# A fused attention and two gated MLPs on one core: the first MLP's token chunks resized, its first chunk fed unnormalised

## The chip, the cores and the metric

The kernel runs on one core of one Trainium2 chip, as one launch. The metric is the device time in microseconds (us) of that core, the median over several executions. Lower is better. The engines are named as in the profile: PE (matrix multiply), PEld (its weight loads, a separate row), DVE (VectorE), ACT (ScalarE), POOL (GpSimd), SP (the queue that issues the DMAs).

## The reference

The input is attention with two kinds of masks, whose output goes through two gated MLPs:

```python
scores = scale * q @ k^T        # batch 4, heads 8, 576 positions, head size 64
# heads 0-3 see the last 32 positions; heads 4-7 every 4th of the last 128
attn_out = softmax(masked scores) @ v
x = attn_out as [2304 tokens, 512]
xn = x / sqrt(mean(x*x, axis=-1) + 1e-6) * rms_g
x  = (silu(xn @ w_gate) * (xn @ w_val)) @ w_out            # 512 -> 1536 -> 512
out = (sigmoid(x @ w_gate2) * (x @ w_val2)) @ w_out2
```

Inputs and outputs are float32; the MLP weights arrive as 64-bit words whose two halves are combined into a float32 on the chip.

## The kernel before

**Numbers.** Every float32 operand of an MLP product is split into a high part that the matrix engine holds exactly (float32r) and the rest. A product is then three matmuls with stationary operands hi, hi, lo (lines 1362 and 1442); each matmul loads its own 128x128 stationary operand.

**First MLP.** The 1536 hidden units are 12 blocks of 128. HOLDS = (6, 6): a first half (pass 0) runs all tokens through blocks 0 to 5, whose weights stay in SBUF, and a second half (pass 1) runs all tokens through blocks 6 to 11 and adds the partial sums. Each half walks over chunks of tokens, `SIZES` in pass 0 and `WIDE` in pass 1, both six chunks of 384. One step of `mlp_step` (one block, one chunk) is 12 matmuls for the gate into bank g, 12 for the value into bank v, an activation and a product on ACT and DVE, and a split into `h`; `y_group` adds 12 matmuls of the step before into four banks y0 to y3. So a chunk costs 6 x 36 = 216 matmuls of the chunk's width, and a half over six chunks 1296.

**Attention and norm.** Attention runs in 48 groups (batch, pair of heads, third of the sequence) that are spread over pass 0. `plan_attention` puts before each chunk the groups that its tokens need: all three groups of the two dilated pairs of every batch that the chunk touches, and the groups of the plain pairs that its tokens lie in. For the six chunks of 384 that is 10, 10, 4, 10, 10, 4 groups. Then `x_norm` squares, sums (line 1067), takes a reciprocal root (lines 1083 to 1108), turns it back by PE (line 1124), scales (line 1147) and splits the chunk (lines 582 to 589). `x_store` writes the split chunk to DRAM for pass 1, one DMA per plane of 128 features and per wide chunk that it overlaps.

**Loads.** q and k of the four pairs of batch 0 come token-major and are turned by PE (`first_qk`, line 796, 16 transposes of 72x72 for one pair, copied out on ACT or DVE). The pairs of the other batches come by `attn_load`: eight DMAs of 72 KB (line 902) and two transposes on DVE (line 916). With `by_pe` = n the first n of those pairs go by `first_qk` instead. MLP weights come through a ring of three buffers `wst` (lines 542, 546): ACT takes an absolute value (line 563), DVE combines the words in four instructions (lines 566, 569, 572, 575), and ACT, POOL or DVE split the result. A `wst` buffer is free when line 575 has read it.

**Second MLP.** It works by a seven-product block scheme on 288-column halves of each batch (lines 1670 and 1593), with sums on DVE, and is not touched.

**Order.** `Line.emit` is a list scheduler that runs when the program is built. It knows engine costs, buffer rings and due times and writes out a fixed order for each engine and for SP. All weights, due times and biases of it are in the dictionary `PARAMS`; `fill_from`, `fill_gap` and `fill_share` say when it puts matmuls on zeros in front of a matmul that it expects to wait.

**Switches that are off before.** With `raw0`, the first chunk isn't scaled by the norm. `plain_split` splits gain times x, and the norm's row is applied behind the products, in pass 0 and once more in pass 1 for the same tokens (a copy of the row is kept in DRAM):

```python
nc.vector.tensor_tensor(out=q.t[:, 0:raw], in0=row.t, in1=gb.t[:, 0:raw], op=ALU.mult)
if raw < T1:
    nc.vector.tensor_copy(out=q.t[:, raw:], in_=gb.t[:, raw:])
...
add("PL", pool(raw), lambda: nc.gpsimd.tensor_tensor(
    out=t.t[:, 0:raw], in0=t.t[:, 0:raw], in1=row.t, op=ALU.mult),
    reads=[("row", "rowm")[p]], writes=[key], tiles=[t, row], due=s + 3.7 * mul,
    other=("x0_lo", "DVE", dves(raw), ...))
```

Chunks of pass 1 that are wider than 384 take parts of their tiles from a second pool (`broad`); nothing else of the arithmetic changes with them.

Of the kernel before, what the change touches and what calls it, by code (L numbers as in the profile page):

```python
# [21 lines left out]


PARAMS = {
    "late": 0, "fill_share": -1.519, "fill_max": 6, "gather": 0.866, "w0_hi": 17.594,
    "w0_lo": 13.068, "h0_hi": 0.512, "h0_lo": -0.096, "x0_hi": 0.96, "x0_lo": 1.138, "ahead": 2,
    "todo0": 464.368, "todo1": 9.635, "todo2": 47.212, "todo3": 0.618, "xb_zero": -1.082,
    "stay": 0.104, "phase": 1.6, "fill_from": 7.028, "fill_gap": -3.039, "margin": 2139.515,
    "wait": 1.172, "w_sq": 3.146, "w_hi": 0.024, "w_lo": 0.907, "x_hi": 0.265, "x_lo": 0.0,
    "h_hi": 7.774, "h_lo": 0.002, "qk": 0.304, "norm": 0.51, "pts": 8.696, "o": 0.0, "snap": 6.738,  # L30
    "h_ahead": 8.667, "h2_ahead": 0.956, "evac": 7.026, "holds": (6, 6), "norm_act": 1.016,
    "slack": 0.0, "share_v": 0.6, "share_p": 0.33, "cold": 1.7, "low": 0, "high": 0.39,
    "recip": 0.3, "rel1": 106.122, "span1": -0.902, "rel2": 17.835, "span2": -0.521, "ys": 0.468,
    "ts": 0.415, "cross": 0.06, "same": 0.04, "dma_lat": 1.7, "dma_rate": 330000.0, "by_pe": 0,
# [3 lines left out]
    "ld_v": -61.445, "ld_c": -66.281, "ld_d": -14.37, "lead": 1.181, "xdue": 12.095,  # L38
    "wdue": -1.028, "wslope": 2.786, "wload": -341.212, "wload_step": 9.03, "warm_n": 36,
    "warm_t": 0.889, "warm_dt": 0.03, "warm_c": 19, "warm_m": 5, "warm_late": -3.526,  # L40
    "warm_due": 32.425, "mask_cost": 0.18, "exp_cost": 0.36, "s_cost": 0.546, "o_cost": 0.41,
    "t_cost": 0.265, "pt_lead": 8.027, "x_lead": 12.171, "wy_due": -0.031, "y_from": 7.985,
    "y_step": 1.502, "xb_due": 0.362, "y_last": 1.346, "xb_last": 6.045, "lo6": 114.359,
    "hi6": 18.752, "sizes": (384, 384, 384, 384, 384, 384), "wide": (384, 384, 384, 384, 384, 384),
    "rush": -0.629, "rush_to": 0.301, "raws": 1, "turns": 2, "raw0": 0,
}
STEP = 6.24

# [1905 lines left out]
```

## Time and profile before

| | us |
|---|---|
| median of 3 runs (1004.35 to 1007.39) | 1005.12 |
| the profiled execution | 1005.76 |
| its span, first to last instruction | 1004.0 |
| PE busy in the span | 974.6 |
| PEld / DVE / ACT / POOL busy | 946.2 / 732.4 / 478.3 / 405.8 |

A busy share is the share of time in which at least one instruction of the engine was in flight. For PE it hides two things: the pipe's latency behind a short burst, and the clock that was granted, which is either 1.2 or 2.4 GHz and is shown as a share of full speed. A stretch with PE busy at a granted clock of 0.80 has 40% of its time at the lower level.

### The profile page before, as it was taken

What the parts mean: (1) busy time and instruction counts of PE and PEld (TensorE: products, weight loads), DVE (VectorE), ACT (ScalarE), POOL (GpSimd) and SP (SyncE); (2) the same over time, 40 slices, a digit from 0 to 9 for tenths busy, and PEclk for the clock granted to TensorE, in tenths of its full rate; (3) what the DMA queues carried; (4) which work ended last, traced back from release to release, by engine and by line L of the source; (5) the groups of instructions that cost most, each with busy time, mean ns of one, the idle gap of its engine ahead of it and who ended that gap; (6) DMA issues with size and microseconds to landing.
All of it is one profiled execution on the core that took longest, in us unless ns stands there. A gap on an engine that the chain in (4) does not pass through costs nothing. (4 is left out here: it accounts for less than half of the span.)

```text
span 1004.0 us, 20084 instructions
## 1 busy us (share of the span) xinstructions
PE 974.6 (97%) x7096; PEld 946.2 (94%) x7096; DVE 732.4 (73%) x1712; ACT 478.3 (48%) x1305; POOL 405.8 (40%) x602
## 2 busy tenths in 40 slices
PE   7898899999999999999999999999999999999997
PEld 6678798998999999999999999999999999999996
DVE  6787897867886888744432569778977688788766
ACT  5976657646432443222221336546654455454432
POOL 5663874443433640010000457337753037661111
PEclk8789799999999999999999999999999999999999
DMA  8858698676779687974662455545276463547634
GB/s 205 191 148 179 134 288 222 155 214 183 236 232 311 228 278 240 331 252 176 234 220 88 136 162 190 210 183 173 69 259 212 156 225 124 189 151 236 161 79 93
DMA packets 213252, 194.53 MB, mean 194 GB/s; under 512 B 137312, under 2 KB 178848, under 8 KB 213152
## 3 DMA queue, kind: packets, MB, share of 16 engines
q1 hardware_dynamic: 213152, 193.25, 63.5%
q8 instruction: 56, 0.92, 0.4%
q14 instruction: 44, 0.36, 0.1%
HBM read 129.50 MB, written 63.70 MB: 192 GB/s over the span
## 5 line engine op out<-in xcount | busy, mean ns | idle before, releaser
L1442 PE MATMUL y<-h,wo 128*128 128x384 f32 x864 | 167.9, 340 | 0.5 <-DVE h L589 0.4
L1362 PE MATMUL g<-xo,w 128*128 128x384 f32 x864 | 165.7, 340 | 0.0
L1362 PE MATMUL v<-xo,w 128*128 128x384 f32 x864 | 162.9, 336 | 0.0
L1442 PEld LDWEIGHTS y<-h,wo 128*128 128x128 f32 x864 | 150.5, 189 | 2.5 <-DVE h L589 0.7
L1362 PEld LDWEIGHTS g<-xo,w 128*128 128x128 f32 x864 | 152.2, 191 | 0.3
L1362 PEld LDWEIGHTS v<-xo,w 128*128 128x128 f32 x864 | 150.2, 188 | 1.3
L582 ACT CAST h<-t 128x384 fp32r<-128x384 f32 (+1 forms) x139 | 65.7, 473 | 111.9 <-DVE t L1410 86.3
L586 POOL TENSOR_TENSOR h<-t,h 128x288 fp32r<-128x288 f32 (+1 forms) x45 | 42.0, 934 | 156.6 <-ACT h L582 151.2
L1410 DVE TENSOR_TENSOR t<-t,v 128x384 f32<-128x384 f32 x72 | 39.6, 550 | 64.0 <-PE v L1362 63.3
L1542 DVE SCALAR_TENSOR_TENSOR pt<-y,pt 128x288 f32<-128x288 f32 x133 | 60.0, 452 | 36.0 <-PE y L1593 33.3
L974 POOL TENSOR_SCALAR pr<-pr,rs 128x96 f32<-128x96 f32 x132 | 57.1, 446 | 56.3 <-DVE rs L969 44.0
L589 DVE TENSOR_TENSOR h<-t,h 128x384 fp32r<-128x384 f32 (+1 forms) x95 | 58.5, 616 | 24.9 <-ACT h L582 23.9
L1593 PE MATMUL y<-h,wo 128*128 128x288 f32 x399 | 72.7, 295 | 0.3 <-ACT h L582 0.2
L586 POOL TENSOR_TENSOR w<-wz,w 128x256 fp32r<-128x256 f32 x58 | 47.3, 830 | 48.5 <-ACT w L582 35.2
L563 ACT ACTIVATE wz<-wst 128x512 f32<-128x512 f32 x72 | 47.9, 669 | 35.1 <-DMA z<-wz 21.7
L1593 PEld LDWEIGHTS y<-h,wo 128*128 128x128 f32 x399 | 59.5, 188 | 0.8 <-ACT h L582 0.5
L586 POOL TENSOR_TENSOR w<-S,w 128x256 fp32r<-128x256 f32 x48 | 38.7, 820 | 52.2 <-DVE w L584 38.0
L572 DVE SCALAR_TENSOR_TENSOR wz<-wst,wz 128x512 int32<-128x512 int32 x72 | 55.8, 775 | 0.9
L961 ACT ACTIVATE pr<-pr,nmx 128x96 f32<-128x96 f32 x144 | 52.4, 366 | 8.0 <-DVE nmx L955 7.7
L575 DVE SCALAR_TENSOR_TENSOR wz<-wst,wz 128x512 int32<-128x512 int32 x72 | 53.2, 738 | 0.6
L1696 ACT ACTIVATE t<-t 128x288 f32<-128x288 f32 x72 | 31.9, 444 | 45.5 <-DVE t L1687 43.9
L586 POOL TENSOR_TENSOR x<-t,x 128x288 fp32r<-128x288 f32 x29 | 27.2, 942 | 64.3 <-ACT x L582 64.3
(231 smaller groups left out, 2112.8 us busy)
## 6 DMA issues: line engine op xcount, KB each, us to landing
z<-wz SPq DMA_DIRECT2D x54, 256.0 KB, 4.7
xo<-xs SPq DMA_DIRECT2D x23, 576.0 KB, 5.7
wst<-in_moe_w_gate_dram SPq DMA_DIRECT2D x24, 512.0 KB, 4.6
wst<-in_moe_w_val_dram SPq DMA_DIRECT2D x24, 512.0 KB, 5.4
wst<-in_moe_w_out_dram SPq DMA_DIRECT2D x24, 512.0 KB, 5.4
xs<-xs SPq DMA_DIRECT2D x21, 576.0 KB, 2.8
wst<-xs SPq DMA_DIRECT2D x18, 576.0 KB, 5.3
x<-xo SPq DMA_DIRECT2D x24, 384.0 KB, 3.2
```

The source lines that it names most:

```text
L563: add("ACT", act(CW), lambda: nc.scalar.activation(out=z.t.bitcast(F32), in_=top().bitcast(F32), func=ACTF.Abs), reads=[("wst", key)], wri ...
L572: add("DVE", Shared(0.595), lambda: nc.vector.scalar_tensor_tensor(out=z.t, in0=top(), scalar=-0x40000000, in1=z.t, op0=ALU.bitwise_and, o ...
L575: add("DVE", Shared(0.595), lambda: nc.vector.scalar_tensor_tensor(out=z.t, in0=low(), scalar=29, in1=z.t, op0=ALU.logical_shift_right, op ...
L582: add("ACT", act(n), lambda: nc.scalar.copy(out=hi(), in_=src()), reads=reads, writes=[key] + [order] * bool(order), tiles=tiles + [dst], ...
L586: add("PL", pool(n), lambda: nc.gpsimd.tensor_tensor(out=lo(), in0=src(), in1=hi().bitcast(F32), op=ALU.subtract), reads=reads, writes=[ke ...
L589: other=(kind + "_lo", "DVE", dves(n), lambda: nc.vector.tensor_tensor(out=lo(), in0=src(), in1=hi().bitcast(F32), op=ALU.subtract)))
L961: add("ACT", PARAMS["exp_cost"], lambda u=u: nc.scalar.activation(out=pr.t[:, u], in_=pr.t[:, u], func=ACTF.Exp, bias=nmx.t[:, u:u + 1], s ...
L974: add("PL", Shared(0.305), lambda u=u: nc.gpsimd.tensor_scalar(out=pr.t[:, u], in0=pr.t[:, u], scalar1=rs.t[:, u:u + 1], scalar2=1.0, op0= ...
L1362: nc.tensor.matmul(out=bank.t, lhsT=w[:, l, cols], rhs=x, start=kk == order[0] and n == 0, stop=kk == order[-1] and n == 2)
L1442: nc.tensor.matmul(out=yb.t, lhsT=w.t[:, l, s], rhs=hs[r].t if broad(p, c) else hs[r].t[:, r], start=n == 0 and j == 0, stop=n == HOLDS[p] ...
L1542: add("DVE", dve(T), lambda: nc.vector.scalar_tensor_tensor(out=t.t[:, e, h], in0=bank.t, scalar=0.5, in1=t.t[:, e, h], op0=ALU.mult, op1= ...
L1593: nc.tensor.matmul(out=bank.t, lhsT=w.t[:, u, a, n], rhs=hs[u].t[:, d], start=first and u == 0 and m == 0, stop=u == NF // 2 - 1 and m == ...
```

## The change

Only `PARAMS` changes. The sizes and switches among it:

- pass 0 in seven chunks, 384, 192, 384, 384, 384, 384, 192, so that the second ends with batch 0 (token 576); the groups before the chunks become 10, 2, 10, 10, 4, 10, 2;
- pass 1 in five chunks, four of 512 and one of 256;
- `raw0` on; `by_pe` = 2, so that the two dilated pairs of batch 1 are turned by PE;
- the scheduler's weights and due times are other ones throughout, those for zero matmuls among them.

```diff
--- before.py
+++ after.py
-    "late": 0, "fill_share": -1.519, "fill_max": 6, "gather": 0.866, "w0_hi": 17.594,
+    "late": 0, "fill_share": -0.39, "fill_max": 6, "gather": 0.153, "w0_hi": 3.206,
...
-    "stay": 0.104, "phase": 1.6, "fill_from": 7.028, "fill_gap": -3.039, "margin": 2139.515,
+    "stay": 0.499, "phase": 1.6, "fill_from": -2.801, "fill_gap": 1.922, "margin": 354.421,
...
-    "ts": 0.415, "cross": 0.06, "same": 0.04, "dma_lat": 1.7, "dma_rate": 330000.0, "by_pe": 0,
+    "ts": 3.186, "cross": 0.06, "same": 0.04, "dma_lat": 1.7, "dma_rate": 330000.0, "by_pe": 2,
...
-    "lo4": 77.56, "hi4": 111.875, "lo5": 139.429, "hi5": 93.074, "ld_a": -87.98, "ld_b": -134.366,
+    "lo4": 46.591, "hi4": 31.519, "lo5": 115.132, "hi5": 121.857, "ld_a": -118.361, "ld_b": -184.2,
...
-    "hi6": 18.752, "sizes": (384, 384, 384, 384, 384, 384), "wide": (384, 384, 384, 384, 384, 384),
-    "rush": -0.629, "rush_to": 0.301, "raws": 1, "turns": 2, "raw0": 0,
+    "hi6": 152.232, "sizes": (384, 192, 384, 384, 384, 384, 192),
+    "wide": (512, 512, 512, 512, 256), "rush": 0.392, "rush_to": 0.976, "raws": 1, "turns": 2,
+    "raw0": 1,
```

## Rows read from the trace of the kernel before

**Rows 1.** The page's slices of the span (40 of 25.1 us): PE and its clock.

```profile
PE   7898899999999999999999999999999999999997
...
PEclk8789799999999999999999999999999999999999
```

**Rows 2.** Busy time by stretch: us; PE, PEld, DVE, ACT, POOL busy (instructions); clock; DMA; GB/s.

```profile
0.00:25.00 25.00, 18.53 (x163) 16.37 (x165) 15.71 (x61) 14.25 (x48) 13.28 (x43) 0.86 0.88 204
25.00:54.00 29.00, 25.55 (x307) 20.76 (x303) 21.21 (x99) 25.33 (x90) 16.77 (x36) 0.76 0.83 189
54.00:64.00 10.00, 7.67 (x79) 5.78 (x80) 9.48 (x39) 8.14 (x30) 6.99 (x14) 0.83 0.27 59
64.00:84.00 20.00, 17.47 (x128) 16.39 (x129) 14.15 (x42) 9.90 (x36) 10.23 (x19) 1.00 0.78 198
84.00:103.00 19.00, 18.53 (x197) 16.46 (x198) 16.96 (x66) 15.32 (x54) 9.17 (x20) 0.91 0.92 178
103.00:130.00 27.00, 23.11 (x168) 21.21 (x167) 24.28 (x68) 17.64 (x58) 24.06 (x40) 0.81 0.66 164
130.00:225.00 95.00, 94.60 (x824) 86.73 (x824) 77.69 (x240) 55.69 (x182) 47.17 (x99) 1.00 0.82 213
```

**Rows 3.** PE in order of time around the first chunk: start, us, instructions, idle before.

```profile
50.91 0.91 PE L1001 MATMUL y<-pts,v 96*64 96x64 f32 x12
...
58.15 0.55 PE L1124 MATMUL y<-ident,rb 128*128 128x128 f32 x3 [1.56 <-DVE rb L1108]
...
63.77 1.85 PE L1362 MATMUL g<-xo,w 128*128 128x384 f32 x9
```

**Rows 4.** PE in order of time, steady: two groups of pass 0, two of the second MLP.

```profile
307.42 2.24 PE L1362 MATMUL g<-xo,w 128*128 128x384 f32 x12
309.50 2.24 PE L1362 MATMUL v<-xo,w 128*128 128x384 f32 x12
...
592.58 1.76 PE L1670 MATMUL att<-wst,w 128*128 128x288 f32 x12
594.18 0.96 PE L1670 MATMUL g<-wst,w 128*128 128x288 f32 x6
```

**Rows 5.** Weight loads after an idle PE, in narrow windows: one load, then two.

```profile
63.77 0.19 PEld L1362 LDWEIGHTS g<-xo,w 128*128 128x128 f32 x1
...
63.77 0.30 PEld L1362 LDWEIGHTS g<-xo,w 128*128 128x128 f32 x2
```

**Rows 6.** Six one-column matmuls in order of time; the group of such: busy us, mean ns.

```profile
44.15 0.83 PE L1067 MATMUL v<-ones,pt 128*128 128x1 f32 x6
...
L1067 PE MATMUL att<-ones,pt 128*128 128x1 f32 x30 | 3.8, 243 | 0.6 <-POOL pt L1059 0.6
```

**Rows 7.** Four PE transposes of 72x72 from `first_qk`.

```profile
27.25 0.47 PE L796 MATMUL g<-ident,pt 72*128 72x72 f32 x4
```

**Rows 8.** DVE in order of time, 51 to 72 us: norm chain, transposes, a weight's words.

```profile
58.51 1.18 DVE L916 STREAM_TRANSPOSE kT<-kraw 128x576 f32<-128x576 f32 x1
59.53 1.08 DVE L1147 SCALAR_TENSOR_TENSOR xn<-xT,gam,y 128x384 f32<-128x384 f32 x2
...
64.74 1.53 DVE L575 SCALAR_TENSOR_TENSOR wz<-wst,wz 128x512 int32<-128x512 int32 x1
...
71.54 0.66 DVE L575 SCALAR_TENSOR_TENSOR wz<-wst,wz 128x512 int32<-128x512 int32 x1
```

**Rows 9.** The DMA queue SP in order of time: issues of weights and of batch 1.

```profile
40.40 0.44 SPq L542 DMA_DIRECT2D wst<-in_moe_w_val_dram  x1
...
41.51 4.13 SPq L902 DMA_DIRECT2D kraw<-in_k_dram  x4
...
49.87 0.44 SPq L542 DMA_DIRECT2D wst<-in_moe_w_gate_dram  x1
...
71.63 0.42 SPq L542 DMA_DIRECT2D wst<-in_moe_w_val_dram  x1
```

**Rows 10.** Busy time at the start of pass 1, columns as in rows 2.

```profile
350.00:360.00 10.00, 10.00 (x60) 10.00 (x59) 9.27 (x15) 4.97 (x10) 7.64 (x8) 1.00 0.46 129
```

More of the change, by code (lines that the diff above doesn't have):

```diff
@@ L24 @@
 PARAMS = {
-    "late": 0, "fill_share": -1.519, "fill_max": 6, "gather": 0.866, "w0_hi": 17.594,
-    "w0_lo": 13.068, "h0_hi": 0.512, "h0_lo": -0.096, "x0_hi": 0.96, "x0_lo": 1.138, "ahead": 2,
-    "todo0": 464.368, "todo1": 9.635, "todo2": 47.212, "todo3": 0.618, "xb_zero": -1.082,
-    "stay": 0.104, "phase": 1.6, "fill_from": 7.028, "fill_gap": -3.039, "margin": 2139.515,
-    "wait": 1.172, "w_sq": 3.146, "w_hi": 0.024, "w_lo": 0.907, "x_hi": 0.265, "x_lo": 0.0,
-    "h_hi": 7.774, "h_lo": 0.002, "qk": 0.304, "norm": 0.51, "pts": 8.696, "o": 0.0, "snap": 6.738,
@@ L40 @@
[L40 to L43, printed above, removed]
-    "hi6": 18.752, "sizes": (384, 384, 384, 384, 384, 384), "wide": (384, 384, 384, 384, 384, 384),
-    "rush": -0.629, "rush_to": 0.301, "raws": 1, "turns": 2, "raw0": 0,
+    "late": 0, "fill_share": -0.39, "fill_max": 6, "gather": 0.153, "w0_hi": 3.206,
@@ new lines @@
+    "w0_lo": 17.529, "h0_hi": 4.676, "h0_lo": 0.63, "x0_hi": 2.311, "x0_lo": 1.214, "ahead": 2,
+    "todo0": 124.924, "todo1": -0.65, "todo2": 638.707, "todo3": -2.959, "xb_zero": -1.296,
+    "stay": 0.499, "phase": 1.6, "fill_from": -2.801, "fill_gap": 1.922, "margin": 354.421,
+    "wait": 16.45, "w_sq": 0.174, "w_hi": 1.13, "w_lo": 1.198, "x_hi": 0.0, "x_lo": 0.374,
+    "h_hi": 0.842, "h_lo": 0.0, "qk": 0.101, "norm": 13.798, "pts": 6.592, "o": 0.0, "snap": 0.298,
+    "h_ahead": 114.386, "h2_ahead": 4.261, "evac": 1.696, "holds": (6, 6), "norm_act": 17.022,
@@ new lines @@
+    "slack": 0.0, "share_v": 0.6, "share_p": 0.33, "cold": 1.7, "low": 0, "high": 0.39,
+    "recip": 0.3, "rel1": -1.107, "span1": -0.522, "rel2": -2.946, "span2": -0.006, "ys": 7.249,
+    "ts": 3.186, "cross": 0.06, "same": 0.04, "dma_lat": 1.7, "dma_rate": 330000.0, "by_pe": 2,
[3 rows of a table added]
+    "ld_v": -39.612, "ld_c": -46.627, "ld_d": -20.824, "lead": -0.396, "xdue": 8.015,
+    "wdue": -1.294, "wslope": 2.482, "wload": -220.1, "wload_step": -0.352, "warm_n": 36,
+    "warm_t": -1.432, "warm_dt": 1.968, "warm_c": 19, "warm_m": 5, "warm_late": -4.274,
@@ L46 @@
+    "warm_due": 0.166, "mask_cost": 0.18, "exp_cost": 0.36, "s_cost": 0.546, "o_cost": 0.41,
+    "t_cost": 0.265, "pt_lead": 7.439, "x_lead": 10.299, "wy_due": 2.299, "y_from": 7.653,
+    "y_step": 1.123, "xb_due": 2.124, "y_last": 0.918, "xb_last": -6.418, "lo6": 123.765,
+    "hi6": 152.232, "sizes": (384, 192, 384, 384, 384, 384, 192),
+    "wide": (512, 512, 512, 512, 256), "rush": 0.392, "rush_to": 0.976, "raws": 1, "turns": 2,
+    "raw0": 1,
 }
```

4 lines of the change are left out of this document (removed), and 4 rows, old and new, of the table PARAMS.

## Prediction

> **What bounds the kernel now.** I read the slices first. They show PE at nine tenths or more nearly everywhere but in the first 125 us and the last slice, and a granted clock under full speed only in the first slices [rows 1]. So the program is matmul-bound from about 130 us on, and what the chunks do there is a matter of how many matmuls there are and how far apart they start. Ahead of 130 us there is waste of two kinds, and the view by stretch gives both [rows 2]. From 54 us, where the last of the ten attention groups for the first chunk has just been multiplied [rows 3], to 130 us PE stood idle for 2.33 + 2.53 + 0.47 + 3.89 = 9.2 us. At a granted clock c a share 2(1 - c) of the time was at 1.2 GHz, and half of the busy time in it is lost: 0.34 x 7.67 / 2 = 1.3, nothing, 0.18 x 18.53 / 2 = 1.7, 0.38 x 23.11 / 2 = 4.4, together 7.4 us. So 16.6 us is the most that the stretch from 54 to 130 can give back. Ahead of 54 us there are 9.9 us of idle time and 7.8 us lost to the clock (0.28 x 18.53 / 2 + 0.48 x 25.55 / 2) [rows 2]; there ACT (25.3 of 29 us) and the DMA (0.83 to 0.88) are the busy ones, so the first ten groups hang on loads and exponentials, which the change leaves in number as they are. From 130 to 225 us PE has 0.4 us of idle time [rows 2], and the last slice, the drain, is busy to seven tenths: up to 7.5 us idle [rows 1].
>
> The profiled execution took 1005.76 us, 0.64 more than the median; its span of 1004.0 leaves 1.8 us around it. I form differences and put them on the median.
>
> **The narrow and the wide matmuls.** In steady flow twelve matmuls of 384 columns start over 2.08 us, 173.3 ns each, and twelve of 288 columns over 1.60 us, 133.3 ns [rows 4]. At 2.4 GHz the columns alone take 160 and 120 ns, so both carry 13.3 ns each. Hence 512 columns cost 226.6 ns and 256 columns 120.0 ns, if nothing else binds. Pass 1: before 1296 x 173.3 = 224.6 us; after 4 x 216 x 226.6 + 216 x 120.0 = 195.8 + 25.9 = 221.7 us; a gain of 2.9 us, all of it on PE's path, since PE has no idle time there [rows 1, 10]. Pass 0: 1080 stay at 384 columns (187.2 us) and 432 have 192 columns. By the same rule one costs 93.3 ns and pass 0 gets 40.3 + 187.2 - 224.6 = 2.9 us longer. The two would cancel: 216 matmuls fewer there, 216 more here.
>
> But each matmul has a 128x128 load. After an idle PE one such load starts with its matmul and the next starts 0.11 us later (two loads span 0.30 us, one lasts 0.19) [rows 5], although the first matmul has 160 ns of columns before it. And six matmuls of a single column with such loads take 0.83 us; less the 0.24 us that one of them lasts, five steps take 0.59 us, 118 ns each [rows 6]. So a load occupies its path for about 110 ns, and 384, 288 or 256 columns cover it while 192 columns (80 ns) don't. I take 112 ns, nearer to the direct row of the load, with 93.3 as the lower end and 121 (load and 13.3 in a row) as the upper. Then the 432 cost 48.4 us and pass 0 is 11.0 us longer; by the ends 2.9 and 14.9. Both halves together: +8.1 us (0 to +12). Half of the 432 belong to the second chunk, which falls into the stretch where PE waits anyway. Of its excess, 216 x 18.7 ns = 4.0 us, I let half disappear there: +6.1. If PE is full there, it is 8.1.
>
> The Trainium skill speaks on both sides of this. "TensorE: Matmul & The Clock Gate", under "LDWEIGHTS (loading the stationary operand)", has a load take its columns over 1.2 GHz, 107 ns for 128, and the rows agree. The same page, under "Weight-path perf modes", says that a faster load comes into play by itself with 128 weights whose type isn't FP32; these operands are float32r. If that held here, the load would hide behind 192 columns, and the third rival below is what would follow; the 0.11 us speak against it.
>
> **The seventh chunk and the transposes on PE.** One more norm is one more trip of six one-column matmuls and three transposes through PE, 0.83 us for the first [rows 6] and 0.55 for the second [rows 3]; of each the last 0.24 us is the way out, which other work covers, so 0.59 + 0.31 = 0.9 us. Two pairs turned by PE are 32 transposes; four take 0.47 us from the first start to the last end [rows 7], so eight times that, 3.8 us, is the upper end, and I take 2.0, since most of a transpose's time is its way out. On DVE that takes away four transposes of about 1.1 us, and on SP 16 issues, of which four hold the queue for 4.1 us between two weight loads [rows 8, 9]; the four larger loads that replace them take part of it back. Sum on PE: +2.9.
>
> **The first chunk without its norm.** Now the tenth group is multiplied at 50.9 us, the root comes back through PE at 58.15, and the first gate products start at 63.77 [rows 3]. The change lets the products follow the attention output by a split alone, so they can start at 53 to 55 us. What it adds on DVE is six multiplications behind the gate bank and four two-operand splits; what it takes away is four scalings. All are two-operand passes over 384 columns and cost about 0.54 us [rows 8]: DVE gets about 3 us more in the first chunk, against 4.4 us that it is spared above. POOL gets six products with the row. The gate bank is single, so the next gate waits for the DVE multiplication, but 24 matmuls (4.2 us) lie between. In pass 1 the same happens once more, over a 512 chunk: six DVE steps of about 0.75 us in a stretch where DVE is at 9.3 of 10 [rows 10]. The gate bank has 24 x 226.6 ns = 5.4 us of cover there; I book nothing, and up to +4.5 us if DVE's queue is late.
>
> **The order of the groups.** This is the part that can pay. Before, the ten groups of the second chunk, eight of them of batch 1, compete with the weights of blocks 2 to 5. The weights of the third block are issued around 40.4 us, but the last DVE instruction of the second of them ends at 66.3 and of the third at 72.2 us, with transposes and scalings of the norm among what DVE does in between; with three buffers, the weight after the one issued at 49.87 goes out at 71.63 [rows 8, 9]. After, two groups are due before the second chunk, and ten more only after 576 tokens' worth of products, 6 x 36 x (173.3 + 112) ns = 61.6 us of PE work. So weights can go first, and long runs of wide matmuls start earlier. PE's own work in the stretch isn't smaller, and weights still need about 2.2 us of DVE each. Between no gain and 16.6 us I take 12.6, leaving 4 us of waste, because with the norm gone and the pressure of batch 1 halved, what is left looks like the stretch from 130 to 225 us, which does the same mixture with 0.4 us idle at full clock [rows 2]. For the time ahead of 54 us I take -1 (+2 to -3): fewer small packets, and zero matmuls that may hold the clock.
>
> **SP and the rest.** Chunks that don't line up with the wide ones make 44 stores of x for 24, and 11 partial sums for 6: 25 more issues at the 0.4 us that a weight's takes [rows 9], 10 us of SP spread over 250 us. Nothing on PE waits for them before pass 1, so nothing is booked. If SP is late, weight loads behind them are. The new order of the second MLP and the tail I book at zero, plus or minus 3, since of what the rows show idle there only the drain can move.
>
> **Sum.** +6.1 + 2.9 - 12.6 - 1 = -4.6, so 1005.1 - 4.6 = 1000.5 us.
>
> **The rivals.** First, slower: the stretch stays as it is because DVE, which must combine twelve weights at 2.2 us beside the attention and now the row products, still sets the pace. DVE is at 24.3 of 27 us from 103 to 130 [rows 2], which speaks for it; that the norm and the transposes leave it speaks against. If only 3 us come back, the time is 1005.1 + 8.1 + 2.9 - 3 = 1013. The point from which it decides is 9 us: with less recovered than 6.1 + 2.9 the change loses. Second, it comes out even: 9 us come back, 1005, between 1002 and 1008. Third, the narrow matmuls cost 93.3 ns: 1005.1 + 2.9 - 12.6 - 1 = 994.4; for it speaks only that no row shows a 192-column matmul. That the products don't start earlier, because weights and not the norm hold them, is part of the first.
>
> **How the numbers follow.** Forecast 0.40 (997 to 1004), slower rival 0.23, even 0.20, cheap narrow matmuls 0.17. About 0.3% (3 us) is what a measurement can tell from no change. Faster: 0.31 of the forecast's 0.40 and all of the third, 0.48. Same: 0.09 and 0.17 of the even case, 0.26. Slower: the first rival and 0.03 of the even case, 0.26. The range from 991 to 1012 leaves out the upper half of the first rival and a full recovery with cheap narrow matmuls (988).
>
> **What would show it.** Groups of twelve 192-column matmuls 1.34 us apart (1.12 would be the third rival). First gate products at 53 to 55 us. PE idle plus clock loss between there and 130 us near 4 us. Pass 1 without idle time, 2.9 us shorter. Wrong would be: the first chunk's steps waiting on weights, PE gaps behind the DVE row products, or a stall where the pass changes.

## Result and profile after

The changed kernel takes 1016.14 us, the median of four executions (1014.27 to 1017.73); the kernel before took 1004.99 us beside it (1004.35 to 1007.39). The ratio is 1.0114, with a 95% interval of 1.009 to 1.0138: the change makes the kernel 11 us slower. Its profiled execution took 1014.27 us with a span of 1012.5. Executions of one kernel lie 2 to 12 us apart in these runs, so two medians of four executions within some 3 us of each other are not told apart below. A figure from one profile carries a scatter of some 3 us as well: *b_wide* (below), whose PE order is that of the kernel before up to 149.8 us, has 41.4 us of the waste defined below by 130 us, where the kernel before has 44.0. Line numbers of the changed kernel are those of before plus one.

The view by stretch, columns as in [rows 2]; the last row is from pass 1:

```profile
0.00:25.00 25.00, 19.50 (x173) 17.54 (x173) 16.74 (x64) 14.28 (x48) 14.29 (x45) 0.80 0.97 212
25.00:54.00 29.00, 24.00 (x234) 20.67 (x231) 21.54 (x89) 22.15 (x74) 17.60 (x36) 0.62 0.77 194
54.00:64.00 10.00, 10.00 (x65) 7.79 (x64) 7.26 (x20) 7.45 (x23) 6.78 (x9) 0.50 0.74 190
64.00:84.00 20.00, 15.53 (x113) 13.84 (x113) 16.71 (x56) 10.96 (x38) 11.64 (x28) 0.84 0.66 181
84.00:103.00 19.00, 18.86 (x170) 17.33 (x169) 13.50 (x47) 12.13 (x41) 16.31 (x27) 0.94 0.63 126
103.00:130.00 27.00, 25.98 (x310) 22.70 (x312) 24.03 (x90) 21.76 (x84) 20.92 (x37) 1.00 0.68 131
130.00:225.00 95.00, 91.06 (x849) 86.19 (x846) 65.53 (x225) 50.36 (x175) 59.97 (x125) 1.00 0.78 188
390.00:590.00 200.00, 200.00 (x943) 168.18 (x942) 112.86 (x193) 50.55 (x93) 45.89 (x38) 1.00 0.69 235
```

Against [rows 2] the waste has moved, not shrunk. The clock is now full from 103 us on, where it was 0.81, but it is 0.62 and 0.50 between 25 and 64 us, where it was 0.76 and 0.83, and PE is idle for 4.5 us between 64 and 84 us and for 3.9 us after 130. By the prediction's own measure the stretch from 54 to 130 has 5.6 us of idle time and 8.6 us lost to the clock, 14.3 us against 16.6, but ahead of 54 us it is 23.5 us against 18.6.

PE in order of time, as in [rows 3]: start, us, instructions, idle before.

```profile
48.09 1.09 PE L1363 MATMUL g<-xo,w 128*128 128x384 f32 x3
...
54.67 1.31 PE L1363 MATMUL g<-xo,w 128*128 128x384 f32 x3
55.91 0.91 PE L1002 MATMUL y<-pts,v 96*64 96x64 f32 x12
56.75 1.33 PE L1363 MATMUL g<-xo,w 128*128 128x384 f32 x3
...
65.93 0.90 PE L1125 MATMUL y<-ident,rb 128*128 128x128 f32 x3 [0.93 <-DVE rb L1109]
66.49 3.61 PE L1363 MATMUL v<-xo,w 128*128 128x384 f32 x12
...
70.72 2.36 PE L1363 MATMUL g<-xo,w 128*128 128x384 f32 x12
...
78.91 0.62 PE L1443 MATMUL y<-h,wo 128*128 128x384 f32 x2 [1.13 <-POOL h L587]
81.94 0.37 PE L1125 MATMUL att<-ident,rb 64*128 64x64 f32 x3 [2.41 <-DVE rs L969]
...
145.77 1.21 PE L944 MATMUL att<-kT,qT 64*64 64x96 f32 x24 [2.64 <-DVE qT L917]
```

The first gate products do start early, at 48.1 us for 63.8. But they come as four groups of three between pieces of attention (one at 61.7 is not shown), and three of 384 columns take 1.3 us. The row of reciprocal roots still goes through PE before the first value products, at 65.9 us, and the second gate starts at 70.7.

PE in order of time in the narrow second chunk:

```profile
171.62 1.50 PE L1363 MATMUL g<-xo,w 128*128 128x192 f32 x12
172.96 1.50 PE L1363 MATMUL v<-xo,w 128*128 128x192 f32 x12
174.30 1.50 PE L1443 MATMUL y<-h,wo 128*128 128x192 f32 x12
```

Twelve products of 192 columns start over 1.34 us, 112 ns each; in [rows 4] it was 2.08 us for 384 columns.

To follow the time through an execution I price every PE instruction at its spacing in steady flow (111 ns for 192 columns, 120 for 256, 133.3 for 288, 173.3 for 384, 226.7 for 512; scores 53, attention values 42, 128x128 transposes 109 ns and so on), add up what has started by a given time, and call the rest of that time the waste. It contains idle time, the clock and bursts that are too short to fill the pipe. The 36 products on zeros that every kernel here starts with count as work.

| waste in us by | 54 | 84 | 130 | 150 | 350 us | pass 1 starts | first MLP ends |
|---|---|---|---|---|---|---|---|
| before | 24.5 | 32.9 | 44.0 | 44.8 | 53.9 | 363.6 | 591.2 |
| after | 27.3 | 40.6 | 44.6 | 48.6 | 54.0 | 377.6 | 601.2 |

Pass 1 starts 14.0 us later with the same waste behind it, as far as one profile tells: the 14.0 us is work. Pass 1 takes 223.6 us for 227.6, and what follows is 1.5 us shorter. 14.0 - 4.0 - 1.5 = 8.5 us, the difference of the two spans. (The medians are 11 us apart because the profiled execution of after was its fastest and that of before lay above its median.)

### The profile page after: what moved, and what is told of

Same layout as the page of the kernel before. It is cut to its first block, busy times and chain, and to the rows that moved or that the text cites. A ratio compares the mean times of both kernels' runs of the same rounds, so it can differ in the third digit from the quotient of the medians.

```text
span 1012.5 us, 20349 instructions
## 1 busy us (share of the span) xinstructions
PE 985.1 (97%) x7137; PEld 925.2 (91%) x7137; DVE 720.9 (71%) x1706; ACT 478.5 (47%) x1338; POOL 440.9 (44%) x639
## 4 chain that ended last, share of the span: by engine, by line
PE 87%; DVE 5%; ACT 3%; DMA 3%; issue 1%; POOL 1%; SPq 0%; ACTq 0%; DVEq 0%; POOLq 0%
PE y L1443 15%; PE g L1363 15%; PE v L1363 14%; PE y L1594 13%; PE att L1671 10%; PE y L1671 5%; PE v L1671 5%; PE g L1671 4%; PE att L944 2%; PE att L1002 1%; DMA wst<-in_moe_w_val_dram 1%; ACT pr L962 1%; DMA wst<-in_moe_w_gate_dram 1%; PE att L989 1%; PE y L1002 1%
## 5 line engine op out<-in xcount | busy, mean ns | idle before, releaser
L1443 PE MATMUL y<-h,wo 128*128 128x384 f32 (+3 forms) x864 | 172.6, 344 | 1.2 <-POOL h L587 1.1
L587 POOL TENSOR_TENSOR h<-t,h 128x288 fp32r<-128x288 f32 (+3 forms) x69 | 67.0, 972 | 216.1 <-ACT h L583 214.0
L1363 PE MATMUL g<-xo,w 128*128 128x384 f32 (+3 forms) x792 | 152.2, 339 | 0.0
L1363 PE MATMUL v<-xo,w 128*128 128x384 f32 (+3 forms) x792 | 150.7, 338 | 0.0
L1363 PEld LDWEIGHTS g<-xo,w 128*128 128x128 f32 x792 | 131.1, 192 | 9.1
L1363 PEld LDWEIGHTS v<-xo,w 128*128 128x128 f32 x792 | 130.2, 191 | 9.0
L583 ACT CAST h<-t 128x288 fp32r<-128x288 f32 (+4 forms) x140 | 66.1, 475 | 118.8 <-DVE t L1411 80.2
L1411 DVE TENSOR_TENSOR t<-t,v 128x384 f32<-128x384 f32 (+3 forms) x72 | 39.7, 551 | 64.2 <-PE v L1363 63.7
L587 POOL TENSOR_TENSOR w<-wz,w 128x256 fp32r<-128x256 f32 x59 | 51.2, 881 | 23.5 <-ACT w L583 22.6
L590 DVE TENSOR_TENSOR h<-t,h 128x288 fp32r<-128x288 f32 (+4 forms) x71 | 44.6, 632 | 16.6 <-ACT h L583 15.4
L1232 DVE TENSOR_TENSOR t<-t,t 128x288 f32<-128x288 f32 x82 | 51.3, 625 | 3.9 <-POOL x L587 1.4
L587 POOL TENSOR_TENSOR w<-S,w 128x256 fp32r<-128x256 f32 x48 | 39.7, 846 | 29.6 <-ACT w L583 20.9
```

The lines of the kernel that those rows point to most:

```text
L583: add("ACT", act(n), lambda: nc.scalar.copy(out=hi(), in_=src()), reads=reads, writes=[key] + [order] * bool(order), tiles=tiles + [dst], ...
L587: add("PL", pool(n), lambda: nc.gpsimd.tensor_tensor(out=lo(), in0=src(), in1=hi().bitcast(F32), op=ALU.subtract), reads=reads, writes=[ke ...
L1232: add("DVE", dves(n), lambda: nc.vector.tensor_tensor(out=dst(), in0=a(), in1=c(), op=ALU.subtract), reads=reads, writes=writes, tiles=til ...
L1363: nc.tensor.matmul(out=bank.t, lhsT=w[:, l, cols], rhs=x, start=kk == order[0] and n == 0, stop=kk == order[-1] and n == 2)
L1443: nc.tensor.matmul(out=yb.t, lhsT=w.t[:, l, s], rhs=hs[r].t if broad(p, c) else hs[r].t[:, r], start=n == 0 and j == 0, stop=n == HOLDS[p] ...
```

## Experiments

**The parts alone, with the scheduler's constants of the kernel before**

*b_wide*: pass 1 in wide chunks, nothing else.

```diff
-    "wide": (384, 384, 384, 384, 384, 384),
+    "wide": (512, 512, 512, 512, 256),
```

> The kernel before with the wide chunks of pass 1 alone (512 four times and 256). If the gain of pass 1 that the trace of after shows (223.4 us from the first gate of pass 1 to the last output product, against 227.4) comes from 216 matmuls fewer at 13.3 ns each and a little of order, the median is about 1001, between 999 and 1003. If the wider tiles only move work, or disturb the order around them, it stays at 1004 or above.

Measured: 1002.77 us (ten executions), ratio 0.9975 [0.9954, 0.9996]. Pass 1 took 224.8 us for 227.6, so this part gives its 2.8 us there. The medians are 1.8 us apart, and the interval just excludes no gain; by them this kernel is the one to keep.

*b_raw*: `"raw0": 0` becomes 1 in the kernel before.

> The kernel before with the first chunk unnormalised, and nothing else. The first gate products should start at 50 to 56 us in place of 63.8. Theory A (the norm holds the first chunk): chunk 1 then starts some 8 us earlier than 129.5 us and the median is 996 to 999. Theory B (the weights of block 5 end the first chunk, at about 125 us in both kernels): chunk 1 starts at 127 to 132 us all the same and the median is 1003 to 1009.

Measured: 1008.47 us, ratio 1.0036 [1.0016, 1.0055]. PE in order of time:

```profile
49.56 1.83 PE L1362 MATMUL g<-xo,w 128*128 128x384 f32 x9
...
63.59 2.37 PE L1362 MATMUL g<-xo,w 128*128 128x384 f32 x12
```

The first gate products come 14 us earlier and the second gate 7 us earlier than the 70.7 of the changed kernel; the waste by 84 us is 30.1 us, 2.8 less than before. By 130 us it is 43.8, the same as before, and the second chunk starts at 129.8 us for 129.5. An early first chunk alone is worth nothing here: what it saves is waited for again ahead of the second chunk. (The profiled execution took 1002.18 us, the fastest of the ten and 6.3 us below their median, so the trace doesn't show where the median's 3.6 us go.)

*a_noraw*: the changed kernel with `"raw0": 1` set back to 0.

> The changed kernel with the norm of the first chunk kept (raw0 at 0) and its new widths: the program that lays out the order makes another order of the first 150 us out of it. Going by my sum, the width of pass 0 costs 10.6 us and pass 1 gives 4.0 us, so with the first stretch as wasteful as before the change (44 us by 130 us) the time is 1011 to 1013 us, 3 us less than the changed kernel (its seventh norm and 32 transposes are not there). Theory that the absent norm does help in this order and only something else takes it away again: the time is 1018 us or more, because the first gate products come at about 64 us again instead of 48 us.

Measured: 1014.62 us, ratio 1.0073 [1.0046, 1.0101]. The seventh norm and the 32 transposes are in this kernel too, against what the expectation says, and PE's order is another one from 39.7 us on. The first gate waits until 68.5 us, the waste by 84 us is 44.4 and by 150 us 46.9 (48.6 in the changed kernel). The first chunk without its norm costs 3.6 us in the old kernel and, by medians that aren't told apart, 1.5 in the new. Its 20 us between 48.1 and 68.5 are covered by attention that has to be done anyway.

**What a narrow product costs**

*a_cols96*: in the changed kernel 400 of the 432 products of 192 columns use 96 of them.

```diff
-nc.tensor.matmul(out=bank.t, lhsT=w[:, l, cols], rhs=x,
+some = 96 if T1 == 192 and not (kk == order[0] and n == 0) else T1
+nc.tensor.matmul(out=bank.t[:, 0:some], lhsT=w[:, l, cols], rhs=x[:, 0:some],
...
```

> The kernel after with 400 of its 432 matmuls of 192 columns cut to 96 columns (the first of each sum keeps 192), so half of those tokens' numbers are left out; the order of every engine is the same. If a 128x128 load of 111 ns sets their pace, nothing changes: 111 ns from start to start, 1014 to 1018. If columns set it, a start to start of 53 ns and some 15 to 23 us less, 993 to 1001.

Measured: 1023.27 us, ratio 1.0157 [1.0107, 1.0206]. PE in order of time, then two stretches as in [rows 2]:

```profile
172.72 1.50 PE L1445 MATMUL y<-h,wo 128*128 128x96 f32 x12
174.06 2.31 PE L1364 MATMUL g<-xo,w 128*128 128x384 f32 x12
...
373.15 2.76 PE L1445 MATMUL y<-h,wo 128*128 128x96 f32 x12
```

```profile
300.00:350.00 50.00, 50.00 (x291) 49.68 (x289) 25.89 (x49) 14.44 (x32) 14.11 (x20) 1.00 0.71 228
350.00:384.00 34.00, 34.00 (x226) 33.90 (x226) 16.39 (x32) 17.26 (x45) 20.94 (x25) 0.76 0.56 179
```

At full clock twelve products of 96 columns take the same 1.34 us (172.72 to 174.06) as twelve of 192. So columns don't set the spacing. That the weight load, which both share, does is shown by the norm's products of a single column: the narrow chunk's norm works on tiles of 64 tokens, so with 128x64 weights. PE of the changed kernel in order of time:

```profile
70.28 0.51 PE L1068 MATMUL att<-ones,pt 128*64 128x1 f32 x6
...
137.58 0.80 PE L1068 MATMUL att<-ones,pt 128*128 128x1 f32 x6 [0.47 <-POOL pr L975]
```

With half the columns of weights the six take 0.29 us less, 58 ns for each of five steps, both at full clock.

In the narrow chunk at 350 us the clock of a_cols96 then fell, to 0.76 for the stretch, where the changed kernel had 1.00 from 344 to 378 us, and groups took twice as long: 0.48 x 34.00 / 2 = 8.2 us lost, where pass 1 starts 5.8 us later. In the narrow chunk before 174 us it had not fallen. Three of the four executions took 1023 to 1025 us at a mean clock of 0.967 to 0.970, and one 1015.36 us at 0.976, so by its clock the one was spared the fall, and its time is that of the changed kernel.

*a_even*: the changed kernel with four chunks of 288 in place of 384 and 192.

```diff
-    "sizes": (384, 192, 384, 384, 384, 384, 192),
+    "sizes": (288, 288, 384, 384, 384, 288, 288),
```

> The kernel after with its two pairs 384+192 cut as 288+288, the same ends of the batches, the same number of matmuls. If a 192-column matmul costs 111 ns because its weight load takes that long, a pair costs 2 x 216 x 133 = 57.6 us in place of 61.4, so 3.8 us less for each pair: 1016 - 7.7, about 1008.5, between 1005 and 1011. If the narrow matmuls are hidden behind other waits in the first stretch, one pair's gain is lost: about 1012. If they cost nothing, 1015 to 1017.

Measured: 1018.71 us, ratio 1.0135 [1.0115, 1.0156]. At 133.3 ns the products of pass 0 need 7.7 us less. But the planner laid out another order: the waste by 350 us is 63.3 us, 9.3 more than in the changed kernel, and pass 1 starts at 379.0, 1.4 us later. What the widths gave, the order took.

*b_ref5, b_end5, b_sizes5, b_all5*: with the constants of the kernel before, the planner finds no order at all for seven chunks. With five of the changed kernel's it does (`qk` 0.101, `lo5` 115.132, `hi5` 121.857, `lo6` 123.765, `hi6` 152.232). So b_ref5 is the kernel before with these five, and the others add to it (`by_pe` stays 0 in all of them):

```diff
-    "sizes": (384, 384, 384, 384, 384, 384),           b_ref5
+    "sizes": (384, 384, 384, 384, 384, 192, 192),      b_end5
+    "sizes": (384, 192, 384, 384, 384, 384, 192),      b_sizes5, b_all5
+    "wide": (512, 512, 512, 512, 256), "raw0": 1,      b_all5
```

> The kernel before with five constants of the order taken from the changed kernel (lead of the q and k turns, due times of the last two blocks' words), widths as before. With these five the order can also be laid out with seven chunks, so this is the reference of the three other runs. Both theories: no meaning of its own, 1003 to 1010 us, as far as the order by chance is a little better or worse than before.

> b_ref5 with one chunk of 384 of pass 0 split into two of 192 at the end, where TensorE is full: (384 five times, 192, 192). Theory W (a product of 192 columns costs 111 ns, held by its weight load): 432 products at 111 ns for 216 at 173.3 ns are 10.5 us more, with the seventh norm's 0.9 us 11.4 us: b_ref5 plus 10 to 13 us. Rival N (the chip starts narrow products closer than 111 ns once they stand beside wide ones, at about 93 ns): plus 2.7 us and the norm, b_ref5 plus 3 to 5 us.

> b_ref5 with the change's sizes of pass 0 (384, 192, four of 384, 192); the first chunk keeps its norm, pass 1 stays at six of 384. Theory W with no gain from the chunk that ends with the batch: b_ref5 plus 10 to 13 us, like b_end5. If a chunk that ends with the first batch lets TensorE run on where it waited (the 12.6 us that I booked come in part from it): b_ref5 plus 0 to 7 us, and below b_end5 by 4 us or more.

> b_ref5 with the whole change except the other constants of the order: the sizes of pass 0, the first chunk without its norm, pass 1 in chunks of 512. From the parts measured alone (wide -2.5 us, no norm +3.6 us, widths as b_sizes5): b_sizes5 minus 2 to plus 2 us. If the absence of the norm pays only together with the new widths, 5 us or more below b_sizes5; if the constants of the changed kernel are what costs, 1005 us or less.

| | median us | waste by 130 | by 350 us | pass 1 starts |
|---|---|---|---|---|
| b_ref5 | 1043.86 (1040.45 to 1050.13) | 45.6 | 87.9 | 397.6 |
| b_end5 | 1059.25 (1056.08 to 1066.88) | 44.2 | 90.9 | 413.9 |
| b_sizes5 | 1037.49 (1033.40 to 1040.53) | 43.4 | 65.9 | 387.6 |
| b_all5 | 1045.03 (1042.24 to 1054.53) | 56.6 | 93.2 | 415.3 |

Waste and starts are those of the profiled execution. The ratios to the kernel before are 1.0407 [1.0349, 1.0465], 1.0554 [1.0501, 1.0607], 1.0324 [1.0279, 1.0368] and 1.0418 [1.0359, 1.0477].

Three things follow. First, the price of the width where PE is full. PE in order of time, b_ref5's sixth chunk, then where b_end5's two narrow chunks start and end:

```profile
360.19 2.24 PE L1362 MATMUL g<-xo,w 128*128 128x384 f32 x12
...
397.63 2.24 PE L1362 MATMUL g<-xo,w 128*128 128x384 f32 x12
```

```profile
364.18 1.48 PE L1362 MATMUL g<-xo,w 128*128 128x192 f32 x12
365.49 1.50 PE L1362 MATMUL v<-xo,w 128*128 128x192 f32 x12
...
413.93 2.27 PE L1362 MATMUL g<-xo,w 128*128 128x384 f32 x12
```

The same 384 tokens take 37.4 us in one chunk and 49.7 in two, 12.3 us more; 10.5 are the 432 x 111 - 216 x 173.3 ns, the rest the seventh norm and its surroundings. The medians give 15.4; by the traces 3.0 us more waste by 350 us is among it. Theory W holds, N falls.

Second, five constants that change not one matmul's size or number cost 39 us, where I had expected 1003 to 1010 us. Up to 130 us b_ref5 has 1.6 us more waste than before; the loss lies behind it, in the second chunk (143 to 214 us) and the third. The stretch from 150 to 250 us of b_ref5 and of b_sizes5, then PE of b_ref5 in order of time:

```profile
150.00:250.00 100.00, 84.76 (x780) 73.76 (x779) 75.90 (x265) 57.18 (x203) 40.72 (x90) 0.88 0.77 210
```

```profile
150.00:250.00 100.00, 95.49 (x792) 90.04 (x791) 74.14 (x224) 46.37 (x144) 30.55 (x62) 0.98 0.75 200
```

```profile
152.14 2.35 PE L1362 MATMUL v<-xo,w 128*128 128x384 f32 x12
...
173.38 2.19 PE L943 MATMUL att<-kT,qT 64*64 64x96 f32 x24 [3.64 <-DVE qT L916]
...
185.18 3.84 PE L1442 MATMUL y<-h,wo 128*128 128x384 f32 x12 [0.64 <-ACT pt L1462]
```

From 154.5 to 185.2 us PE multiplies attention alone, and no product of the MLP.

Third, what the chunk that ends with the batch is good for. b_sizes5 has 22.0 us less waste by 350 us than b_ref5 (87.9 to 65.9) for its 10.5 us of products, and it is 22 us faster than b_end5, which pays for the same widths. That is what the idea promised, but the rows don't show the idea at work. By the plan 20 groups are due before b_ref5's second chunk and 24 before its third; the values of 27 were done at 154.5 us, and the nine that follow in one piece up to 185.2 us are due only before the fourth. So b_ref5 loses time to the place that its order gave them, and b_sizes5 has another order beside its other widths: which of the two gave the 22 us, no run separates. The kernel before has little such waste: 0.8 us from 130 to 150 and 9.1 us from there to 350. The sum of the parts fails for b_all5: by the medians it is 7.5 us slower than b_sizes5, and it has 13 us more waste by 130 us (its profiled execution is its slowest, 9.5 us above the median). On these constants the order laid out with the absent norm makes the first stretch worse.

**What holds the first stretch**

a_half and b_half get another order by their edit. The others keep the order of their kernel on PE and on SP, a_fillers too, which only adds products on zeros; differences are theirs alone. The waste by 84, 130 and 150 us stands against its 40.6, 44.6 and 48.6.

*a_norow*: the first chunk's gate bank doesn't wait for the row.

```diff
-nc.vector.tensor_tensor(out=q.t[:, 0:raw], in0=row.t, in1=gb.t[:, 0:raw], op=ALU.mult)
+nc.vector.tensor_copy(out=q.t[:, 0:raw], in_=gb.t[:, 0:raw]) if not p else ...
```

> The changed kernel, order untouched, with one edit: the gate bank of the first chunk is copied out without the row of reciprocal roots, so that the bank does not wait for the row (the gate values of that chunk are then not normalised). In the changed kernel the first product with the row ends at 67.8 us and the second gate group starts at 70.7 us, no earlier than before. Theory R (the norm still stands in the way, now as the condition for the gate bank to come free): the second gate group starts some 5 us earlier, the waste by 84 us falls from 40.6 us to 36 us or less, and the time falls to 1010 to 1013 us. Theory A (the engines behind the attention's softmax hold the stretch up to 130 us, whatever the row does): the second gate group comes earlier, the waste by 130 us stays within 1.5 us of 44.6 us, and the time stays at 1015 to 1018 us.

Measured: 1017.21 us, ratio 1.0092 [1.0063, 1.0122]; waste 39.9, 43.9 and 48.0. PE in order of time:

```profile
65.36 0.90 PE L1125 MATMUL y<-ident,rb 128*128 128x128 f32 x3 [0.93 <-DVE rb L1109]
65.91 3.65 PE L1363 MATMUL v<-xo,w 128*128 128x384 f32 x12
...
70.18 2.35 PE L1363 MATMUL g<-xo,w 128*128 128x384 f32 x12
```

The second gate comes 0.5 us earlier, not 5, and so does all that stands ahead of it (the first gate starts at 47.56 us for 48.09). Theory R falls: the bank isn't what is late. The way of the row through PE stands in PE's written order ahead of the first value products, and PE waits there as before, 0.93 us; that wait no run took away.

*a_words*: two of the four DVE instructions that combine a weight's words are left out in pass 0.

```diff
-add("DVE", Shared(0.33), lambda: nc.vector.tensor_scalar(      # twice
+add("DVE", Shared(0.33), lambda: p and nc.vector.tensor_scalar(
```

> The kernel after without two of the four DVE instructions for the words of the 18 weights of pass 0 (the lower bound and the shift), so those weights are not the right numbers; the written order of every engine is the same. DVE is spared some 0.85 us for each weight, 15 us in all ahead of 125 us. Theory B1 (DVE sets the pace at which weights arrive): the last gate and value of chunk 0 come 5 to 10 us earlier than 128.2 us and the median falls to 1006 to 1011. Theory B2 (the order holds them, behind attention groups and DMA issues placed ahead of them): under 2 us, 1014 to 1016.

Measured: 1016.39 us, ratio 1.0113 [1.0089, 1.0137]; waste 39.7, 42.9 and 46.5. DVE's words don't set the pace.

*a_half, b_half*: blocks 3 to 5 use the weights of blocks 0 to 2, whose loads, words and splits fall away, in the changed kernel and in the kernel before.

```diff
+            if f >= 3:
+                for key, src in (...):
+                    line.writer[key] = line.writer[src]
...
+                continue
```

> The kernel after with the same nine weights left out. Its waste is 27.3 us by 54, 40.6 by 84, 44.6 by 130 and 54.0 by 350: from 84 to 130 only 4 us. Theory S: the products of the first chunk run on once they have started, the waste at 84 falls by 6 to 10 us, the median is 1004 to 1009. Theory H: the first gate bank still waits for the norm's row at about 67 us and for the attention ahead of it; under 4 us less, 1012 to 1016.

> The kernel before with nine weights in place of 18 in pass 0: blocks 3 to 5 use the weights of blocks 0 to 2, so the numbers are not the right ones, and the loads, words and splits of nine weights fall away. The waste of PE (time less matmul work at full clock) is 24.5 us by 54 us, 44.0 by 130 and 53.9 by 350. Theory S (the turn of the three load buffers, about 20 us for the three weights of a block, ends the first chunk): chunk 1 starts at 105 to 115 us in place of 129.5, the waste at 130 falls by 8 to 12 us, the median is 993 to 998. Theory H (attention and its engines hold the stretch): chunk 1 by 122 to 130, under 3 us less, 1002 to 1006.

Measured: 1019.55 us, ratio 1.0145 [1.0112, 1.0178], and 1042.35 us, ratio 1.0379 [1.0343, 1.0415]. With work taken away the planner lays out other orders, so neither is a clean test. In a_half the second chunk starts at 128.0 us, 7.5 earlier, but 8.1 us of waste come back between 150 and 200 us. b_half looks like b_ref5: waste 88.6 us by 350. Both say that a better supply of weights isn't by itself a gain, and the second, with the constants' 39 us, how far an order can fall.

*a_fillers*: `fill_share` of the changed kernel from -0.39 to 0.45, so that more products on zeros keep PE busy where it waits: 77 of them, all ahead of 75 us, in an otherwise unchanged order.

> The kernel after with more matmuls on zeros ahead of matmuls that are expected to wait (fill_share 0.45). The clock was granted at 0.62 from 25 to 54 us, 0.50 from 54 to 64, 0.84 from 64 to 84, a loss of up to 16.6 us of busy time. If the clock is what holds the early products, it rises to 0.9 or more there, the waste without the zero matmuls by 84 us falls by 5 to 10 us and the median is 1007 to 1012. If the stretch hangs on attention's chain and the loads, the clock rises and the time stays at 1014 to 1018, or gets longer by the zero matmuls in the way.

Measured: 1022.39 us, ratio 1.0181 [1.0141, 1.0221]. By stretch, then PE in order of time:

```profile
25.00:54.00 29.00, 25.52 (x299) 21.65 (x300) 21.88 (x97) 22.30 (x81) 15.51 (x30) 0.88 0.73 179
54.00:64.00 10.00, 7.40 (x80) 5.75 (x81) 8.75 (x22) 7.89 (x23) 6.92 (x12) 1.00 0.62 179
```

```profile
52.35 0.69 PE L1363 MATMUL g<-xo,w 128*128 128x384 f32 x3
...
74.77 2.24 PE L1363 MATMUL g<-xo,w 128*128 128x384 f32 x12
```

The clock is bought back (0.88 and 1.00 for 0.62 and 0.50), and the waste by 84 us, with the 77 counted in, is 42.2, not less: PE now spends 54 to 64 us with 2.6 us of idle time and with products on zeros. The first gate starts 4.3 us and the second 4.1 us later than in the changed kernel, and the same instructions are 3.4 us late at 15 us already (2 to 5 us in between). So the higher clock carries PE through the stretch no sooner: what it gives goes into waiting and into the zeros, and the low clock is in the main a sign of waiting and not its cause.

*a_noexp, a_noexp0, b_noexp*: the softmax's exponential, its sum's reciprocal and the normalisation are left out, for batches 1 to 3 (a_noexp, b_noexp) or batch 0 (a_noexp0).

```diff
-add("ACT", PARAMS["exp_cost"], lambda u=u: nc.scalar.activation(
+add("ACT", PARAMS["exp_cost"], lambda u=u: b or nc.scalar.activation(
...
```

> The changed kernel, order untouched, without the softmax's exponential on ScalarE, its sum's reciprocal, and its normalisation for the batches 1 to 3 (the TensorE instructions are all there; attention of those batches is not normalised and not exponentiated). Theory A (TensorE waits in 54 to 150 us for the chain scores, exponential, normalisation, transposes of the attention): the waste by 150 us falls from 48.6 us by 8 us or more, and the time to 1004 to 1009 us. Rival (the order of the instructions and the arrival of words and weights hold it): the waste by 150 us falls by less than 3 us, and the time stays at 1013 to 1017 us.

> The changed kernel, order untouched, without the softmax's exponential, its sum's reciprocal and its normalisation for the first batch alone (whose twelve attention groups end at 64 us in the changed kernel). Theory A0 (ScalarE's exponentials and the normalisation of the first batch hold the first 84 us): the waste by 84 us falls from 40.6 us by 5 us or more, and the time to 1008 to 1011 us. Rival: the waste by 84 us falls by less than 2 us and the time stays at 1013 to 1018 us.

> The same work left out of the kernel before (exponential, reciprocal and normalisation of batches 1 to 3), order untouched. Theory A: its waste by 130 us falls from 44.0 us by 6 us or more, and the time to 995 to 999 us. Rival: the waste falls by less than 3 us and the time stays at 1002 to 1006 us. If this kernel gains and the changed one does not, the changed order is held by something else than the kernel before.

Measured: a_noexp 1017.88 us, ratio 1.0105 [1.0081, 1.0129], waste 40.4, 44.1 and 50.2. a_noexp0 1014.86 us, ratio 1.0097 [1.0071, 1.0122], waste 39.7, 43.4 and 49.7. b_noexp 1003.34 us, ratio 0.9975 [0.9954, 0.9996], waste 47.3 by 130 us for 44.0. ACT loses a third of its busy time (21.8 to 13.8 us from 103 to 130 in a_noexp) and PE gains nothing that these medians tell; b_noexp's is 2 us lower, while its profiled execution, 1007.76 us, is its slowest. Theories A and A0 fall, in both kernels.

*a_alloff*: the last three together, for all batches: no softmax work behind the maximum, half of the words, no product of the first gate with the row.

> The changed kernel, order untouched, with three of its works left out together: the softmax's exponential, reciprocal and normalisation of all batches, two of the four VectorE operations of each word of pass 0, and the product of the first chunk's gate with the row. Theory C (several engines are late one behind the other, so that each alone gains nothing): the waste by 130 us falls from 44.6 us by 8 us or more, and the time to 1004 to 1009 us. Rival D (TensorE's own order, the transfers and the clock hold it): the waste by 130 us falls by less than 3 us, and the time stays at 1012 to 1017 us.

Measured: 1013.38 us, ratio 1.008 [1.0056, 1.0103]; waste 35.9, 38.7 and 45.0. Neither theory is right as it stood. By 130 us 5.9 us are gained, so the engines do hold PE a little, one behind the other; then 6.3 us are lost by 150 us, where the changed kernel loses 4.0. What PE waits for there, and what that waits for, in order of time on SP, DVE and PE:

```profile
126.41 7.99 SPq L856 DMA_DIRECT2D v<-in_v_dram  x13
134.51 2.20 SPq L903 DMA_DIRECT2D qraw<-in_q_dram  x4
...
138.78 0.78 DVE L917 STREAM_TRANSPOSE qT<-qraw 128x576 f32<-128x576 f32 x1 [3.07 <-DMA qraw<-in_q_dram]
...
139.71 2.19 PE L944 MATMUL att<-kT,qT 64*64 64x96 f32 x24 [3.64 <-DVE qT L917]
```

The q of a pair is issued behind two lots of thirteen small loads of v, at 0.6 us of the queue each. The changed kernel has the same sequence:

```profile
122.83 7.77 SPq L856 DMA_DIRECT2D v<-in_v_dram  x13
130.69 2.02 SPq L903 DMA_DIRECT2D kraw<-in_k_dram  x4
132.82 7.72 SPq L856 DMA_DIRECT2D v<-in_v_dram  x13
140.65 2.16 SPq L903 DMA_DIRECT2D qraw<-in_q_dram  x4
...
144.85 0.78 DVE L917 STREAM_TRANSPOSE qT<-qraw 128x576 f32<-128x576 f32 x1 [2.08 <-DMA qraw<-in_q_dram]
```

Added up over such rows, SP issues for 25.7 of the 30 us from 100 to 130 and for 21.0 of the 22 us from 130 to 152 in the changed kernel (28.0 and 16.3 in the kernel before, where it also issues for 28.1 of the 30 us from 54 to 84). So the next thing that is late, once the engines are relieved, seems to be the queue that issues the loads. That is read from the traces; no run took issues away from SP, and that part stays open.

## Why the prediction was wrong

The forecast was 1000.5 us, on the wrong side. Term by term:

| term | forecast | measured |
|---|---|---|
| narrow products, pass 0 | +11.0, less 2.0 hidden | +10.5, nothing hidden |
| wide products, pass 1 | -2.9 | -4.0 (-2.8 in b_wide) |
| seventh norm, transposes on PE | +2.9 | +3.4 (the remainder: 14.0 less 10.5 and 0.1) |
| order of the groups and ahead of 54 us | -12.6 - 1 | +0.1 (waste 53.9 to 54.0) |
| second MLP and tail | 0 | -1.5 |
| sum | -4.6 | +8.5 by the spans |

Of the remainder of 3.4 us, the 32 transposes (64 ns each in steady flow) and the norm's own products come to 2.2. Another 0.75 us moves between two rows: pass 0's last output group, twelve products, runs behind the first products of pass 1 and has 192 columns where it had 384. Without it pass 1 is 3.3 us shorter, nearer to the 2.8 of b_wide.

**The products.** The rule of 13.3 ns beside the columns gave 226.6 and 120.0 ns; measured are 226.8 and 120. For 192 columns the choice of 112 ns from the spacing of two loads was right (111), and both ends (93.3 and 121) were wrong. The third rival, 93.3 ns, falls. The Trainium skill, "TensorE: Matmul & The Clock Gate", under "LDWEIGHTS (loading the stationary operand)", has a load take its columns over 1.2 GHz, 107 ns for 128 by that formula, and the 111 ns agree; the faster load of its section "Weight-path perf modes" was not seen, as a_cols96 shows with 111 ns for 96 columns as well. That half of the second chunk's excess would disappear in waiting time was wrong: the second chunk's products ran 112 ns apart in steady flow, and what PE waited there (2.64 us at 145.8) came on top.

**The step that failed** is "the order of the groups", the -12.6 us, with "the first chunk without its norm" ahead of it. It had three links. (1) Products start at 53 to 55 us: they started at 48.1, earlier than forecast. (2) Early products turn waiting time into work: they didn't. b_raw shows it in the old kernel (2.8 us gained by 84 us, no more than the scatter, and 0.2 left by 130), and a_noraw in the new one (20 us later, no slower). In the changed kernel the early products moved ahead of attention that was then late itself: the twelfth group of scores and values ended at 64 us for 57, and the waste by 84 us rose by 7.7 us. (3) What is left will look like the stretch from 130 to 225 us, since eight groups fewer are due before the second chunk. That was an argument by likeness and no reading. Both kernels have 24 groups through by 130 us (27 by their scores): the attention has to be done for the later chunks, whatever the second chunk itself needs, and the planner put it where it was. The waste by 130 us is 44.0 and 44.6 us, and between 41.4 and 47.3 in every run that kept the order of one of the two, or set `raw0` or the wide chunks in it, but for a_alloff (38.7) and, by its added zeros, a_fillers. I had the waste right (16.6 us by the rows from 54 to 130) and took it for something that the sizes would give back. It stayed with the written order and what feeds it. (The 7.8 us of clock loss ahead of 54 us was also miscounted there; its terms give 8.7.)

**Whether the mechanism exists** stays open. b_sizes5 is 22 us faster than b_end5, but its order is another one, and the waste that it is spared lies in and behind the second chunk, where b_ref5's order had made it. The rows of before had next to none there (0.4 us idle from 130 to 225), and I had read that row as the state to reach, not as a sign that there was nothing to be had.

**The first rival** gave 1013 us, near the 1016, and its point of decision holds: 9 us had to come back, and by the prediction's measure 2.3 did from 54 to 130 us, with 4.9 lost ahead of it. Its reason was wrong, since DVE's words are not the pace (a_words), so that the time came near it is luck. What holds the stretch is settled only in part. It is not the gate bank's wait for the row, nor the words, nor the exponentials, each alone, and a clock bought back with zeros gave nothing (a_fillers); the first three together are worth 6 us by 130, of which 3 are left at the end, no more than medians tell apart. The rest lies with the order and the queue of loads, which these runs don't separate. Nor did any run give the six old chunks the changed kernel's constants, or switch `by_pe` alone, so what the constants and what the sizes did to the order stays open too.

Of the signs named, the groups of 1.34 us came, pass 1 was without idle time, and the 4 us of waste didn't come; PE gaps behind the row's products and a stall where the pass changes didn't either.

## What to carry to other kernels

Where an order is written out by a planner with many constants, a gain that needs a better order is no term of a sum: here five constants moved the time by 39 us while the new widths cost 10. Cost the products, which can be had to a microsecond from the spacing of steady groups, and book a recovered stall only where the trace shows the waiting instruction, the thing that it waits for, and that the change takes away just that. Count the work that the stretch must do in either order, and look at the queue that issues the loads as at an engine, because no busy share shows it.

## What the runs showed of the hardware

- Products of 128x128 float32r weights start 111 ns apart with 192 and with 96 columns (after, a_cols96), and products of one column 112 ns apart with 128x128 weights and 58 ns with 128x64 (after): the load sets the pace. From 256 columns on it is the columns at 2.4 GHz and 13.3 ns (120, 133.3, 173.3 and 226.8 ns for 256, 288, 384 and 512).
- With 96 columns the granted clock fell to 0.76 in a stretch in which PE had no idle time by the records (34.00 of 34.00 us); with 192 columns at the same place it was 1.00. I had expected a PE without gaps to keep its clock. The other narrow chunk of the same execution kept it, and one of four executions took some 8 us less at a higher mean clock (0.976 for 0.967 to 0.970).
- With 77 more products on zeros and the order unchanged the clock of 54 to 64 us rose from 0.50 to 1.00, and PE came through the stretch no sooner (a_fillers).
